# Router logits by float32 matmuls in four column tiles, on tokens that are not split in two

## The chip, the cores and the metric

The kernel runs on one core of a Trainium2 chip. The time is the device time of one execution in microseconds; three executions of the kernel before took 1358.14 to 1362.7 us, median 1361.56. The core's engines are TensorE (PE in the profile, its weight loads PEld), VectorE (DVE), ScalarE (ACT), GpSimd (POOL) and SyncE (SP, which here only issues transfers). Each works through its own queue in order; semaphores tie them.

## The reference

Two steps. The first is a causal average over 7 positions in each of 8 heads, with the softmax of a small table as weights:

```
x_pad = concat([zeros(B, 6, 192), x])                 # x is 8 x 3584 x 192
out[b,s,h,:] = sum_k softmax(weight)[h,k] * x_pad[b, s+k, h, :]
```

The second routes the 28672 results, called tokens, to 8 experts and applies a two-layer network:

```
logits = x @ w_gate                                   # 28672 x 8
for idx in argsort(-logits.flatten()):                # best pair first
    tok, e = idx // 8, idx % 8
    if assigned[tok] < 0 and counts[e] < 3584: assign tok to e
out[tokens of e] = relu(x[tokens of e] @ w1[e]) @ w2[e]   # 192 -> 1024 -> 192
```

Every token ends with exactly one expert, and every expert with 3584 tokens. Which expert a token gets hangs on comparisons between logits, so these have to be as exact as float32.

## The kernel before

**Attention and logits.** The tokens go in 16 batches of 1792 (half a sequence), 16 windows of 112 positions each. `load(i)` brings batch i into a tile X of 118 partitions (112 positions and the 6 before them); there are three such tiles, and the load for batch i+2 is issued on SP's queue at the top of batch i. `conv(i)` runs over the 8 heads h: one float32 matmul with a banded matrix TH into one of four PSUM banks "cv", then ACT copies the bank to the tile a (two of them), and after head 7 ACT's queue sends a to the scratch tensor attn in device memory. Between the matmul and the copy of each head, `mid(h)` puts the other work of the batch into the engines' queues:

- at h = 0 to 3, `transp(i-1, h)`: DVE transposes 32 x 32 blocks of a quarter of the batch before (a to aT), which puts features on partitions;
- at h = 2 to 5, `split(i-1, h-2)`: ACT rounds the quarter to the reduced format float32r (hi), and POOL, or DVE for the last quarter of some batches and in batch 15, subtracts (lo = aT - hi);
- at h = 0 and h = 4, `logits(i-2, 0)` and `(i-2, 1)`: 6 float32r matmuls of 512 columns each, hi with the table GH and lo with GL, all into one bank pl. GH holds the rounded gate weights in 32 columns and what the rounding left in another 32, so a bank has two halves that are added at the end.

After head 7, `end(i-2)` turns the logits round: ACT copies pl to L, PE transposes L in four pieces into a bank pt, DVE adds the two halves into the table LT with two operations, and `top` takes each token's best logit (M). Batch 15 is different: `transp_last` moves it in three thirds, and its logits come from plain float32 matmuls with the 32-column table GF (in the wk tile "c_mu"), six of 512 columns into partitions 0 to 31 of a bank.

**Routing** runs in the background, as generators whose steps `hook()` puts between the steps of the foreground. `half(0)` finds a threshold on the tokens seen so far by counting (`thresh`: DVE operations on X, m_x and t_t, and a small PE matmul per round), takes the first 8 batches, and makes lists of tokens for each expert: `sort` makes one-hot tiles oa on DVE (128 x 1024, bf16) and multiplies them on PE (128 matmuls bg<-X,oa), `gather` and `tokens` finish the list ia. The first expert tile's tokens are gathered with it (xg<-attn, on POOL's queue). `tail` does the logits of batch 14 and `tail2` those of batch 15, both after the last convolution, between the first expert matmuls; `half(1)`, `rest` and `last` route the remainder during the experts.

**What sets the order.** All queues are written in program order at build time; nothing is reordered on the chip. `hook` decides with a model of three clocks (`Meter`, `Pace`): every operation on PE, DVE and ACT adds an estimated time to its engine's clock, and a background step is put in when DVE's clock is not more than a slack ahead of PE's and what the step needs is past. So a change of what the model counts moves background steps to other places.

**Experts.** `FFN.run` goes over 56 tiles of 512 tokens: gather, transpose, `l1` (five float32r matmuls per 128 hidden units into ph), ReLU on ACT and the remainder on DVE (hh, hl), `l2` (into y), and a scatter. Weights are split once (`wsplit`: ACT rounds, POOL or DVE subtracts), which starts in batch 15 at heads 4 and 5, and written back to device memory for later use.

Of the kernel before, what the change touches and what calls it, by code (L numbers as in the profile page):

```python
# [5 lines left out]
F32 = mybir.dt.float32  # L6
# [21 lines left out]
class Meter:  # L28
# [5 lines left out]
    def __getattr__(self, op):  # L34
        f = getattr(self.eng, op)
        if op == "dma_start":
            return f

        def call(*a, **k):
            p = self.pace  # L40
            aps = [t for t in (*a, *k.values()) if hasattr(t, "shape") and hasattr(t, "dtype")]
            n = max(map(size, aps), default=0)
            bf = all(t.dtype == BF for t in aps if size(t) > 1)
            if self.name == "pe":
                n = size(aps[2])
# [7 lines left out]
            return f(*a, **k)  # L53

        return call
# [56 lines left out]
def build(ctx, tc, nc, x, weight, wg, attn, LT, wk):  # L112

    k = K()
# [44 lines left out]
    wgr = cst.tile([128, 6, 8], F32, name="wgr")  # L159
    GH = cst.tile([128, 6, 128], FR, name="GH")  # L160
    GL = cst.tile([128, 6, 128], FR, name="GL")
    GF = wk.tile([128, 6, 32], F32, name="c_mu")
    pm = wk.tile([128, 16], F32, name="pm")

    def gate_ops():
        for pb in range(4):
            nc.sync.dma_start(wgr[32 * pb:32 * pb + 32], wg.rearrange("(c f) e -> f c e", f=32))
        P.memset(GH.bitcast(F32), 0.0)
        P.memset(GL.bitcast(F32), 0.0)
        for pb in range(4):  # L170
            q = slice(32 * pb, 32 * pb + 32)
            P.tensor_copy(GH[q, :, 8 * pb:8 * pb + 8], wgr[q])
            P.tensor_copy(GL[q, :, 8 * pb:8 * pb + 8], wgr[q])
            P.tensor_tensor(GH[q, :, 32 + 8 * pb:40 + 8 * pb], wgr[q], GH[q, :, 8 * pb:8 * pb + 8].bitcast(F32),
                            op=OP.subtract)
        P.tensor_tensor(GF, GH[:, :, 0:32].bitcast(F32), GH[:, :, 32:64].bitcast(F32), op=OP.add)

# [33 lines left out]
    def transp(i, u):  # L211

        if u == 0:
            AT[i] = ([], k.hp[i % 2].tile([128, 16, 6, 32], FR, name="hi"),
                     k.hp[i % 2].tile([128, 16, 6, 32], FR, name="lo"))
        aT = k.tp.tile([128, 4, 6, 32], F32, name="aT%d" % u)
        V.transpose(aT.rearrange("p w c t -> p (w c t)"), AA[i][:, 4 * u:4 * u + 4].rearrange("p w d -> p (w d)"))
        AT[i][0].append(aT)
        if u == 3:
            AA.pop(i)  # L220

    def split(i, u, eng):
        aT = AT[i][0][u]
        hi, lo = (t[:, 4 * u:4 * u + 4] for t in AT[i][1:])
        A.activation(hi, aT, AF.Copy)
        eng.tensor_tensor(lo, aT, hi.bitcast(F32), op=OP.subtract)  # L226

# [7 lines left out]

    def logits(i, part):
        _, hi, lo = AT[i][0:3]
        if part == 0:
            AT[i] = (None, hi, lo, k.bank("pl"))
        pl = AT[i][3]  # L240
# [3 lines left out]
        if part:  # L244
            L = AT[i] = k.lrow()
            A.activation(L, pl[0:64], AF.Copy)

    def logits_last(u):
        i = NHB - 1
        if u == 0:  # L250
            AT[i].insert(0, k.bank("pl"))
        pl = AT[i][0]
        a = AT[i][1 + u].rearrange("p w (c t) -> p w c t", t=32)
        for c in range(2):
            PE.matmul(pl[0:32], GF[:, 2 * u + c], a[:, :, c], start=(u + c == 0), stop=(u + c == 3))
        if u == 2:
            L = AT[i] = k.lrow()
            A.activation(L[0:32], pl[0:32], AF.Copy)

    def logits_t(i):  # L260
        L = AT.pop(i)
        pt = k.bank("pt")
        last = i == NHB - 1
        n = 32 if last else 64
        for b in range(4):
            PE.transpose(pt[:, 64 * b:64 * b + n], L[0:n, 128 * b:128 * b + 128], k.ident[0:n, 0:n])
        v = pt[:, 0:256].rearrange("p (b s q e) -> p s e b q", s=2, q=4, e=8)
        o = LT[:, :, 16 * i:16 * i + 16].rearrange("p e (b q) -> p e b q", q=4)
        V.tensor_tensor(o, v[:, 0], pm.rearrange("p (b q) -> p b q", q=4)[:, None].to_broadcast([128, 8, 4, 4]),
                        op=OP.add)  # L270
        if not last:
            V.tensor_tensor(o, o, v[:, 1], op=OP.add)

    k.load, k.conv, k.transp, k.split, k.logits, k.logits_t = load, conv, transp, split, logits, logits_t
    k.toeplitz, k.gate_ops, k.transp_last, k.logits_last = toeplitz, gate_ops, transp_last, logits_last
    return k

# [1074 lines left out]
def moe_kernel(ctx, tc, x, weight, wg, w1, w2, out):  # L1352
# [6 lines left out]
    with ExitStack() as cw:  # L1359
# [46 lines left out]
        def tail():  # L1406

            k.logits(14, 0)
            k.logits(14, 1)
            yield PEA  # L1410
            end(14)
# [5 lines left out]
        def tail2():  # L1417
            for u in range(3):
                k.logits_last(u)
                yield PEA if u == 2 else None  # L1420
            end(15)
# [4 lines left out]
        bg.keep = 5  # L1426
        cs, c1, ct, ca, cl, cc = (ExitStack() for _ in range(6))
        cx = [ExitStack() for _ in range(3)]
# [3 lines left out]
        k.hp = [pool(cs, "hp0", 1, **right), pool(c1, "hp1", 1, **right)]  # L1432
        k.tp = pool(ct, "tp", 1, **right)
        k.ap = pool(ca, "ap", 2, **right)
# [5 lines left out]
        k.bank = lambda name: lps.tile([128, 512], F32, name=name)  # L1440
        k.lrow = lambda: lp.tile([64, 512], F32, name="L")

# [23 lines left out]
        for i in range(NHB):  # L1466
# [49 lines left out]
        end(13)  # L1516
        for c in (ca, ct, c1, cl):
            c.close()
        k.bank = lambda name: r.bg()
        k.lrow = lambda: oh.tile([64, 512], F32, name="oa")  # L1520
        ff.py = pool(cw, "py", 2, space=PSUM, **late)
# [66 lines left out]
```

## Time and profile before

| | |
|---|---|
| median of three runs | 1361.56 us (1358.14 to 1362.7) |
| the profiled execution | 1359.7 us, its span from first to last instruction 1357.9 us |
| PE, DVE, ACT, POOL busy | 94%, 78%, 43%, 47% of the span |
| hi on ACT, lo on POOL and DVE | 60 x 0.842, 50 x 1.893 and 10 x 1.648 us |
| transposes aT on DVE | 60 x 0.950 us |
| logit matmuls hi and lo of batches 0 to 13 | 84 and 84 |

Times in the profile are microseconds from the span's start. A row of a group names the line of the program (here nearly always 53, the helper that records every operation), engine, operation and tiles as out<-in, shapes, how often, busy time with the mean of one in ns, and the idle time of the engine just before with what ended it. PE's records overlap, since a matmul starts before the one ahead has ended: the mean is a latency, and what one costs is seen in how far apart they start. A float32 matmul leaves two records, one in float32r leaves one. A row of the timeline gives the start, the length of a merged stretch and how many records it holds. In the tables of stretches, the numbers after the engines' busy times are PE's granted clock as a share of full, the share of time in which the 16 transfer engines are busy, and GB/s.

### The profile page before, as it was taken

To read this page: it belongs to the slowest core of one execution; us is meant where nothing else is said; L and a number is where in the kernel's file an instruction comes from. 1 tells how busy PE (TensorE), PEld (TensorE's weight loads), DVE (VectorE), ACT (ScalarE), POOL (GpSimd) and SP (SyncE) were. 2 spreads that over 40 slices of the span, in tenths; PEclk is the share of its full clock that TensorE was granted. 3 is DMA by queue.
4 is the path that set the end of the run, shared out by engine and by line. 5 is a ranking of instruction groups with operands and counts; after the bars stand their busy time and mean duration, and the time that the engine had idled before them with its cause. 6 is when DMAs were issued, how large, how long until landed. Compare 5 with 4: busy or idle time off the path is not lost.

```text
span 1357.9 us, 20887 instructions
## 1 busy us (share of the span) xinstructions
PE 1282.5 (94%) x7351; PEld 1099.0 (81%) x7351; DVE 1055.2 (78%) x2248; ACT 587.7 (43%) x1242; POOL 636.1 (47%) x607
## 2 busy tenths in 40 slices
PE   5878896999889999999999999999999999999997
PEld 3544564788778898888889999999999999999997
DVE  7698964777999898898775777777777777777772
ACT  4655464357543444353324333333333333333332
POOL 5555557457664344344224434444443444444422
PEclk9988898999989999999989999999999999999999
DMA  9996569658764334324224241324322314141110
GB/s 228 287 257 191 167 211 297 206 176 288 258 224 155 122 110 144 134 94 139 78 71 145 95 173 58 101 91 145 100 87 85 101 47 145 45 146 41 42 33 28
DMA packets 114431, 188.23 MB, mean 139 GB/s; under 512 B 12352, under 2 KB 86544, under 8 KB 110096
## 3 DMA queue, kind: packets, MB, share of 16 engines
q1 hardware_dynamic: 63888, 120.75, 28.0%
q0 software_dynamic: 21504, 44.07, 10.6%
q10 hardware_dynamic: 28928, 22.02, 4.9%
q8 instruction: 59, 0.97, 0.3%
q14 instruction: 52, 0.43, 0.1%
HBM read 114.44 MB, written 72.35 MB: 138 GB/s over the span
## 4 chain that ended last, share of the span: by engine, by line
PE 73%; DVE 15%; DMA 4%; issue 3%; POOL 2%; ACT 2%; SPq 0%; POOLq 0%; DVEq 0%; ACTq 0%
PE ph L53 34%; PE y L53 33%; DVE X L53 4%; PE bg L53 3%; DMA attn<-a 2%; DVE aT L53 2%; DVE oa L53 2%; DVE hl L53 1%; PE cv L53 1%; DMA raw<-in_moe_w_dram 1%; POOL w L1187 1%; PE px L53 1%; DVE TH L53 1%; POOL xg L1206 1%; ACT hi L53 1%
## 5 line engine op out<-in xcount | busy, mean ns | idle before, releaser
L53 PE MATMUL y<-w,hh 128*128 128x384 f32 x1792 | 542.8, 358 | 0.0
L53 ACT ACTIVATE hh<-ph 128x512 fp32r<-128x512 f32 x448 | 267.6, 598 | 497.5 <-PE ph L53 497.4
L53 DVE SCALAR_TENSOR_TENSOR hl<-ph,hh 128x512 fp32r<-128x512 f32 x448 | 308.0, 688 | 185.1 <-ACT hh L53 181.4
L53 PE MATMUL y<-w,hl 128*128 128x192 f32 x1792 | 450.6, 251 | 0.0
L53 PE MATMUL ph<-xa,w 128*128 128x512 f32 x1344 | 399.1, 405 | 7.1 <-POOL w L1187 3.7
L53 PEld LDWEIGHTS y<-w,hh 128*128 128x128 f32 x1792 | 338.7, 189 | 25.2 <-issue 7.4
L53 PEld LDWEIGHTS y<-w,hl 128*128 128x128 f32 x1792 | 343.2, 192 | 15.3
L1274 POOL DMA_INDIRECT out_dram<-yo,ib x128 | 126.7, 990 | 295.6 <-DVE yo L53 280.7
L53 PEld LDWEIGHTS ph<-xa,w 128*128 128x128 f32 x1344 | 221.1, 191 | 29.2 <-DVE hl L53 4.0
L1274 POOL DMA_INDIRECT out_dram<-yo,ia x96 | 105.0, 1094 | 247.1 <-DVE yo L53 214.8
L53 DVE STREAM_TRANSPOSE xs<-xg 32x256 f32<-32x256 f32 (+1 forms) x512 | 188.8, 369 | 8.8
L53 PE MATMUL ph<-xd,w 128*128 128x512 f32 x448 | 179.2, 400 | 0.3 <-ACT w L53 0.3
L53 PE MATMUL ph<-xd,dl 128*128 128x512 f32 x448 | 175.8, 392 | 1.6 <-DVE dl L53 1.6
L1206 POOL DMA_INDIRECT xg<-attn,ib x128 | 129.5, 1012 | 40.1 <-issue 39.8
L226 POOL TENSOR_TENSOR lo<-aT,hi 128x768 fp32r<-128x768 f32 x50 | 93.3, 1893 | 74.4 <-ACT hi L53 74.4
L53 PE MATMUL cv<-X,TH 118*128 118x384 f32 x256 | 108.6, 558 | 18.9 <-DVE TH L53 12.4
L1206 POOL DMA_INDIRECT xg<-attn,ia x96 | 108.7, 1133 | 28.8 <-issue 24.3
L53 ACT ACTIVATE yt<-y 128x192 f32<-128x192 f32 x224 | 73.5, 328 | 109.0 <-PE y L53 107.4
L53 DVE TENSOR_TENSOR yo<-y,yt 128x192 f32<-128x192 f32 x224 | 79.5, 355 | 42.9 <-ACT yt L53 40.1
L53 PEld LDWEIGHTS cv<-X,TH 118*128 118x128 f32 x256 | 51.2, 213 | 65.5 <-issue 14.6
L53 PEld LDWEIGHTS ph<-xd,dl 128*128 128x128 f32 x448 | 84.9, 190 | 22.6 <-DVE dl L53 3.0
L53 PEld LDWEIGHTS ph<-xd,w 128*128 128x128 f32 x448 | 84.9, 190 | 21.1 <-issue 1.3
(243 smaller groups left out, 1191.7 us busy)
## 6 DMA issues: line engine op xcount, KB each, us to landing
w<-kw SPq DMA_DIRECT2D x16, 1536.0 KB
w<-kv SPq DMA_DIRECT2D x16, 1536.0 KB
X<-in_x_dram SPq DMA_DIRECT2D x16, 1344.0 KB
attn<-a ACTq DMA_DIRECT2D x16, 1344.0 KB
kw<-w SPq DMA_DIRECT2D x48, 256.0 KB
kv<-w SPq DMA_DIRECT2D x32, 384.0 KB
raw<-in_moe_w_dram SPq DMA_DIRECT2D x32, 192.0 KB
raw<-in_moe_w_dram SPq DMA_DIRECT2D x16, 256.0 KB
```

Source lines behind the costliest of these rows:

```text
L53: return f(*a, **k)
L226: eng.tensor_tensor(lo, aT, hi.bitcast(F32), op=OP.subtract)
L1187: eng.tensor_tensor(lo, r[0:n], hi[0:n].bitcast(F32), op=OP.subtract)
L1206: self.nc.gpsimd.indirect_dma_start(out=t[:, b], out_offset=None, in_=self.attn[0:rows], in_offset=bass.IndirectOffsetOnAxis(ap=idx[b], ax ...
L1274: st = nc.gpsimd.indirect_dma_start(out=self.out, out_offset=bass.IndirectOffsetOnAxis(ap=idx, axis=0), in_=o, in_offset=None, bounds_chec ...
```

## The change

Batches 0 to 14 are no longer split. The transposes write straight into one float32 tile aT per batch; hi, lo, the tables GH and GL, their pool, and the four splits are gone. GF, the 32-column table, now serves all batches. `logits(i, u)` takes feature block u of 6: four matmuls, one for each group of four windows, each 128 partitions by 32 weight columns with 128 tokens moving, and each writing its own 32 partitions of the bank (a column tile of the array). A batch has 24 of them, 12 at h = 2 and 12 at h = 5. The result has the four groups on four quarters of the partitions, so L is 128 x 128, one transpose turns it, and one DVE operation puts it into LT. Batch 15 uses the same function on its three thirds. The model of clocks counts such a matmul as a quarter of a float32 one, with its lower limit of 0.107 us.

```diff
-                d = n / 2400 * (1 if aps[2].dtype in (BF, FR) else 2 if op == "transpose" else 4)
+
+                d = n / 2400 * (1 if aps[2].dtype in (BF, FR) or size(aps[1]) == 32 else 2 if op == "transpose" else 4)
...
-        P.memset(GH.bitcast(F32), 0.0)
-        P.memset(GL.bitcast(F32), 0.0)
+        P.memset(GF, 0.0)
         for pb in range(4):
             q = slice(32 * pb, 32 * pb + 32)
...
+            P.tensor_copy(GF[q, :, 8 * pb:8 * pb + 8], wgr[q])
...
-        aT = k.tp.tile([128, 4, 6, 32], F32, name="aT%d" % u)
-        V.transpose(aT.rearrange("p w c t -> p (w c t)"), AA[i][:, 4 * u:4 * u + 4].rearrange("p w d -> p (w d)"))
-        AT[i][0].append(aT)
+            AT[i] = [k.hp[i % 2].tile([128, 16, 6, 32], F32, name="aT")]
+        V.transpose(AT[i][0][:, 4 * u:4 * u + 4].rearrange("p w c t -> p (w c t)"),
+                    AA[i][:, 4 * u:4 * u + 4].rearrange("p w d -> p (w d)"))
...
-    def split(i, u, eng):
-        aT = AT[i][0][u]
-        hi, lo = (t[:, 4 * u:4 * u + 4] for t in AT[i][1:])
-        A.activation(hi, aT, AF.Copy)
-        eng.tensor_tensor(lo, aT, hi.bitcast(F32), op=OP.subtract)
...
-        g, t = ((GH, hi), (GL, lo))[part]
-        for fb in range(6):
-            PE.matmul(pl, g[:, fb], t[:, :, fb, :], start=(part == 0 and fb == 0), stop=(part == 1 and fb == 5))
...
+        for c in range(4):
+            w = slice(4 * c, 4 * c + 4)
+            t = AT[i][u // 2].rearrange("p w (c t) -> p w c t", t=32)[:, w, u % 2] if i == NHB - 1 else AT[i][0][:, w, u]
+            PE.matmul(pl[32 * c:32 * c + 32, 0:128], GF[:, u], t, start=(u == 0), stop=(u == 5))
+        if u == 5:
             L = AT[i] = k.lrow()
-            A.activation(L, pl[0:64], AF.Copy)
...
+        PE.transpose(pt[:, 0:128], L, k.ident)
+        v = pt[:, 0:128].rearrange("p (b q e) -> p e b q", q=4, e=8)
         o = LT[:, :, 16 * i:16 * i + 16].rearrange("p e (b q) -> p e b q", q=4)
...
-                if i and 2 <= h < 6:
-                    k.split(i - 1, h - 2, V if h == 5 and (i < 6 or i == 14) or i == 15 else P)
-                if 2 <= i and h == (2 if i == 2 else 0):
-                    k.logits(i - 2, 0)
-                if 2 <= i and h == 4:
-                    k.logits(i - 2, 1)
+                if 2 <= i and h in (2, 5):
+                    for u in range(3):
+                        k.logits(i - 2, h // 4 * 3 + u)
```

How this stands in the queues. On PE, the end of routing's first half (the matmuls iq and c_oh, from which the list of tokens comes) before, at the start of batch 14; cv are the convolution's matmuls, pl the logits, px the transposes of the first expert tile:

```order
L53 MATMUL pl<-hi,GH 128x512 x6
L53 LDWEIGHTS ones
L53 MATMUL bg<-iq,ones 128x192
...
L53 MATMUL bg<-c_oh,X_1528 128x24
L53 MATMUL cv<-X,TH 128x384 x4
L53 MATMUL pl<-lo,GL 128x512 x6
L53 MATMUL cv<-X,TH 128x384 x3
L53 MATMUL pt<-ident,L 128x64 x4
L53 MATMUL cv<-X,TH 128x384
L53 MATMUL pl<-hi,GH 128x512 x6
```

and with the change, inside batch 15, up to the first expert tile:

```order
L54 MATMUL pl<-aT,c_mu 32x128 x12
L54 LDWEIGHTS ones
L54 MATMUL bg<-iq,ones 128x192
...
L54 MATMUL bg<-c_oh,X_1547 128x24
L54 MATMUL cv<-X,TH 128x384 x3
L54 MATMUL pl<-aT,c_mu 32x128 x12
L54 MATMUL cv<-X,TH 128x384 x2
L54 MATMUL px<-ident,xg 128x128 x4
```

Before, a whole batch follows iq ahead of px; now 5 convolution matmuls and 12 logit matmuls do. On POOL, where the last batch passes into the experts, before:

```order
L226 TENSOR_TENSOR lo<-aT_1635,hi 128x768
L1206 DMA xg<-attn,ia_105 128x192 x8
L1109 MEMSET dl 64x1024
L1187 TENSOR_TENSOR w_1763<-raw,w_1763 128x512
L1187 TENSOR_TENSOR dl<-raw,w_1763 64x512
```

and with the change:

```order
L1078 MEMSET dl 64x1024
L1156 TENSOR_TENSOR w_1629<-raw,w_1629 128x512
L1156 TENSOR_TENSOR dl<-raw,w_1629 64x512
L1175 DMA xg<-attn,ia_105 128x192 x8
L1156 TENSOR_TENSOR w_1629<-raw,w_1629 128x512
```

The subtraction lo is gone from POOL, and the memset and the first two weight splits now stand ahead of the eight gathers.

More of the change, by code (lines that the diff above doesn't have):

```diff
@@ L234, in transp_last, with logits @@
         AT[i] = AT[i] + [a] if u else [a]
[L236 to L240, printed above, removed]
-        g, t = ((GH, hi), (GL, lo))[part]
-        for fb in range(6):
-            PE.matmul(pl, g[:, fb], t[:, :, fb, :], start=(part == 0 and fb == 0), stop=(part == 1 and fb == 5))
-        if part:
-            L = AT[i] = k.lrow()
-            A.activation(L, pl[0:64], AF.Copy)
[L248 to L258, printed above, removed]
+    def logits(i, u):
+        if u == 0:
+            AT[i].append(k.bank("pl"))
+        pl = AT[i][-1]
+        for c in range(4):
[3 more added lines that the diff above has]
+        if u == 5:
+            L = AT[i] = k.lrow()
+            A.activation(L, pl[:, 0:128], AF.Copy)
     def logits_t(i):
@@ L262, in logits_t @@
         pt = k.bank("pt")
[L263 to L267, printed above, removed]
-        o = LT[:, :, 16 * i:16 * i + 16].rearrange("p e (b q) -> p e b q", q=4)
[L269 to L275, printed above, removed]
+        PE.transpose(pt[:, 0:128], L, k.ident)
+        v = pt[:, 0:128].rearrange("p (b q e) -> p e b q", q=4, e=8)
+        o = LT[:, :, 16 * i:16 * i + 16].rearrange("p e (b q) -> p e b q", q=4)
+        V.tensor_tensor(o, v, pm.rearrange("p (b q) -> p b q", q=4)[:, None].to_broadcast([128, 8, 4, 4]), op=OP.add)
+    k.load, k.conv, k.transp, k.logits, k.logits_t = load, conv, transp, logits, logits_t
+    k.toeplitz, k.gate_ops, k.transp_last = toeplitz, gate_ops, transp_last
     return k
@@ L1406, in tail @@
         def tail():
-            k.logits(14, 0)
-            k.logits(14, 1)
-            yield PEA
+            for u in range(6):
+                k.logits(14, u)
+                if u % 2:
+                    yield PEA if u == 5 else None
             end(14)
@@ L1417, in tail2 @@
         def tail2():
-            for u in range(3):
-                k.logits_last(u)
-                yield PEA if u == 2 else None
+            for u in range(6):
+                k.logits(15, u)
+                if u % 2:
+                    yield PEA if u == 5 else None
             end(15)
@@ L1426, in moe_kernel @@
         bg.keep = 5
-        cs, c1, ct, ca, cl, cc = (ExitStack() for _ in range(6))
+        cs, c1, ca, cl, cc = (ExitStack() for _ in range(5))
         cx = [ExitStack() for _ in range(3)]
```

16 lines of the change are left out of this document (3 added, 13 removed).

## The prediction

> **What bounds the kernel now.** I read first the page's 40 slices of 34 us, for where the engines are full, and then the same by stages.
>
> ```profile
> span 1357.9 us, 20887 instructions
> PE   5878896999889999999999999999999999999997
> DVE  7698964777999898898775777777777777777772
> PEclk9988898999989999999989999999999999999999
> DMA  9996569658764334324224241324322314141110
> ```
>
> ```profile
> 12.00:75.00 63.00, 56.45 (x180) 33.28 (x181) 42.19 (x82) 38.08 (x76) 38.30 (x53) 0.97 1.05 279
> 75.00:205.00 130.00, 107.88 (x487) 68.03 (x486) 112.95 (x186) 72.46 (x138) 73.80 (x44) 0.87 0.69 202
> 205.00:285.00 80.00, 68.11 (x417) 51.84 (x416) 50.80 (x101) 31.52 (x63) 45.90 (x41) 0.91 0.74 240
> 285.00:1357.90 1072.90, 1050.07 (x6274) 945.83 (x6273) 841.54 (x1856) 439.78 (x952) 473.37 (x454) 0.99 0.35 115
> ```
>
> The columns are the stretch, its length, busy time of PE, weight loads, DVE, ACT and POOL, then the granted clock, the DMA share and GB/s. From 285 us on PE is busy 1050 of 1073 us: the expert stage is PE's, and this change leaves it alone. So what is won or lost comes before 285 us. There, 12 to 75 us has DMA full (share 1.05, 279 GB/s), and 75 to 205 us has DMA down to 202 GB/s, PE with gaps at clock 0.87, and DVE busy 113 of 130 us. The loads of x mark the batches: the load for batch i+2 is issued when the convolution of batch i-1 ends, so these three rows are the starts of batches 2, 5 and 13.
>
> ```profile
> 28.25 0.27 SPq L194 DMA_DIRECT2D X<-in_x_dram  x1
> 58.23 0.27 SPq L197 DMA_DIRECT2D X<-in_x_dram  x1
> 170.31 0.27 SPq L197 DMA_DIRECT2D X<-in_x_dram  x1
> 204.53 0.66 PE L53 MATMUL px<-ident,xg 128*128 128x128 f32 x4 [1.60 <-ACT a L53]
> X<-in_x_dram SPq DMA_DIRECT2D x16, 1344.0 KB
> attn<-a ACTq DMA_DIRECT2D x16, 1344.0 KB
> ```
>
> Batches 2 to 4 take (58.2 - 28.3) / 3 = 10.0 us each, batches 5 to 12 take (170.3 - 58.2) / 8 = 14.0 us, batches 13 to 15 end on PE at 204.5 - 1.6 = 202.9, so 32.6 us together. A batch moves 2 x 1344 KB and a 70 KB piece of x, 2.82 MB; at 290 GB/s (between the 279 above and the peak slice) that is 9.7 us. Batches 2 to 4 run at that pace. Batches 5 to 12 do not, and there the question is who holds them.
>
> ```profile
> ACT hi L53 <- DVE aT L53: 11.2, 6, 2.8
> PE bg L53 <- DVE m_x L53: 10.2, 3, 3.8
> L53 DVE TENSOR_TENSOR oa<-irep,q 128x1024 bf16<-128x1024 bf16 x16 | 19.6, 1263 | 0.7 <-PE bg L53 0.7
> L53 DVE TENSOR_TENSOR oa<-irep,q 128x1024 bf16<-128x1024 bf16 x33 | 21.0, 681 | 0.0
> L53 DVE TENSOR_SCALAR X<-X,t_t 128x576 bf16<-128x576 bf16 x6 | 7.5, 1298 | 0.0
> L53 DVE TENSOR_SCALAR X<-X,t_t 128x384 bf16<-128x384 bf16 x9 | 2.3, 313 | 0.1
> L53 DVE SCALAR_TENSOR_TENSOR t_t<-t_u,t_t 128x1 f32<-128x1 f32 x12 | 7.3, 636 | 0.3
> L53 DVE TENSOR_REDUCE t_u<-t_mx 128x1 f32<-128x3 f32 x5 | 0.8, 156 | 0.2
> L53 DVE TENSOR_TENSOR lo<-aT,hi 128x768 fp32r<-128x768 f32 x5 | 5.4, 1103 | 0.3 <-ACT hi L53 0.3
> L53 DVE TENSOR_TENSOR LT<-LT,pt 128x128 f32<-128x128 f32 x9 | 2.6, 287 | 0.3
> L226 POOL TENSOR_TENSOR lo<-aT,hi 128x768 fp32r<-128x768 f32 x50 | 93.3, 1893 | 74.4 <-ACT hi L53 74.4
> L53 ACT ACTIVATE hi<-aT 128x768 fp32r<-128x768 f32 x60 | 50.5, 842 | 22.3 <-DVE aT L53 22.3
> ```
>
> (Waits are of 75 to 125 us; the oa row of 16 is of 75 to 206 us, that of 33 from 285 us on.) DVE sets the pace in two ways. Its own work is long, and partly swollen: the same oa takes 1263 ns here and 681 later, and an operation on one element per partition takes 636 ns where a neighbour takes 156. POOL runs lo for 93 us in just this stage, so I read the swelling as DVE waiting while POOL works; the trace shows the coincidence, not the cause. And DVE is tied into PE's path through ACT: hi of the batch before stands in ACT's queue between the evacuations a<-cv, so a late transpose stops them, and four banks later PE.
>
> **The change part by part.**
>
> *Removed.* All 60 hi on ACT (50.5 us), all 50 lo on POOL (93.3) and 10 on DVE, the second LT addition, and the tie just named: ACT keeps only a<-cv and L, and what waits for aT is now a matmul two thirds of a batch later. In 75 to 205 us DVE loses 5.4 (lo) and 2.6 (LT), and if the swelling is POOL's, 16 x (1.263 - 0.681) = 9.3 from oa, 6 x (1.298 - 0.313 x 1.5) = 5.0 and 12 x (0.636 - 0.156) = 5.8 from the threshold: 28 us of its 113. That leaves 85 us for some 10.5 batches, 8.1 each, under DMA's 9.7. If the swelling stays it is 105, 10.0 each, 0.3 over DMA's pace and 2.4 us over eight batches. So DVE falls to about DMA's pace or below it either way.
>
> *Added on PE.* Six passes hi and six lo per batch, 128 columns wide, become 24 float32 matmuls of 32 by 128, in the trace two records each, 48 records.
>
> ```profile
> 186.37 1.42 PE pl L53 x6
> 19.43 5.40 PE L53 MATMUL cv<-X,TH 118*128 118x384 f32 x16 [0.38 <-DVE TH L53]
> 237.42 3.62 PE L53 MATMUL bg<-X,c_mu 128*32 128x512 f32 x8
> 237.88 0.11 PEld L53 LDWEIGHTS bg<-X,c_mu 128*32 128x32 f32 x1 [0.32 <-issue]
> 205.03 0.60 PE L53 MATMUL bg<-ident,xg 128*64 128x128 f32 x4
> 363.89 0.20 PE L53 MATMUL bg<-onesf,r_c 128*8 128x1 f32 x2
> 180.39 1.65 PE L53 MATMUL bg<-X,oa 128*128 128x16 bf16 x24
> L53 PE MATMUL bg<-onesf,r_c 128*8 128x1 f32 x14 | 1.4, 166 | 0.0
> ```
>
> Now: the convolution is (5.40 - 0.49) / 15 = 0.327 a record, 5.2 us for 16, its own latency of 0.49 taken off. Logits are 2 x 1.42 = 2.84, four transposes about 0.4: 8.5 us a batch. No row shows four column tiles at once. Upper bound: one after the other, as the 128-column float32 records of ident,xg come, (0.60 - 0.27) / 3 = 0.109 apart, 48 x 0.109 = 5.2 us. Lower bound: as near as two float32 records ever follow here, 0.20 - 0.166 = 0.03, 48 x 0.032 = 1.5 us. The two are far apart and the four tiles write four different quarters of the partitions, so I take the middle by ratio, 2.8 us. One transpose is 0.15 and I allow 0.4 for changing between whole array and tiles: 8.55 us a batch. PE's load thus stays as it was, 8.5, and under DMA's 9.7.
>
> [...]
>
> *Moved.* The planner puts the first half of routing one batch later: sorting (128 matmuls oa at (1.65 - 0.21) / 23 = 0.063, 8 us) from batches 12 and 13 to 13 and 14, its end from the start of batch 14 into batch 15. On POOL two weight splits now stand ahead of the first eight gathers.
>
> *Sum against the profiled 1359.7 us.* Batches 0 to 4 are DMA's and stay. Batches 5 to 12 at 9.7 are 77.6 instead of 112.1: -34.5. Batches 13 and 14 at 8.55 + 4.0 and 15 at 8.55 + 2.0 are 35.7 instead of 32.6: +3.1. PE waited 10.2 us for the threshold's m_x in its order; I leave about half, +6. Stage: -25.4. After it, the logits of batches 14 and 15 stand on PE's path between the first experts' matmuls: 2.84 and 12 x 3.62 / 8 = 5.4 become 2 x 2.8, -2.6. Nothing else in PE's 1050 us moves. Sum -28, so 1331.7 in the profile's own time; the median of the runs is 1.9 above that execution, which gives 1334.
>
> **The rivals.** *The tiles do not run side by side* (the change not doing what it says). 5.2 us of logits make a batch 10.95: batches 2 to 4 +2.9, 5 to 12 are 87.6 (-24.5), 13 to 15 are 42.9 (+10.3), stalls +6, after the stage 10.4 - 8.2 = +2.2. Sum -3, 1358 us. For it: every float32 record in the trace pays its columns in full. Against: those all use the same columns of the array.
>
> *Each record waits for its own weights*, on the slower side. Place: the 768 records, 672 in the 14 batches and 96 after; price 0.11 + 0.107 = 0.217 each, 10.4 a batch, which is then 16.1: batches 2 to 4 +18, 5 to 12 +17, 13 to 15 +26, after the stage 20.8 - 8.2 = +13. 1436 us. It decides from 0.113 us a record, where the gain of 3 us above is used up. Against it: eight c_mu records with their own 0.11 us loads come (3.62 - 0.59) / 7 = 0.43 apart, and 512 columns at the 0.109 of 128 would be 0.436, so there the loads are hidden.
>
> [...]
>
> *The late list gives back part.* The first gather needs the list, which in this order ends with 5 convolutions and 12 logit matmuls to go, 5.3 us.
>
> ```profile
> 187.63 0.26 PE L53 MATMUL bg<-iq,ones 128*128 128x192 bf16 x1
> 190.11 0.19 DVE L53 SCALAR_TENSOR_TENSOR ia<-m_j,m_x 128x32 int32<-128x32 int32 x1
> PEld ph L53 <- POOL w L1187: 4.0, 1, 4.0
> xg<-attn,ia POOLq DMA_INDIRECT x96, 2.8
> ```
>
> From that iq matmul to the list is 2.7 us, four gathers at about 1.3 are 5.2, landing 2.8: 10.7 us, so PE stands idle 5.4. Against: the two splits ahead of the gathers can take away PE's 4.0 us wait for POOL's w, which is why the sum has neither. With the full 13 us of threshold stalls instead of 6 it is +12: 1346 us.
>
> *DMA's pace to the end.* If sorting hides too, batches 5 to 15 at 9.7 are 106.7 instead of 144.7; with -2.6 and the 4.0 of w that is -45, 1317 us. Against: PE's 12.6 in batches 13 and 14.
>
> **How the numbers follow.** The forecast 0.40 (1324 to 1344 on its own), late list 0.28, no overlap 0.18, DMA's pace 0.10, waiting for weights 0.04. The three faster cases are 0.78. No overlap lies about the edge of 0.3% (4 us, what a measurement of this kernel tells from nothing): 0.07 faster, 0.08 the same, 0.03 slower. So faster 0.85, same 0.08, slower 0.07. The range runs from just below DMA's pace to just below no overlap, 1315 to 1357, leaving out half of that case, the weights and a little below.
>
> **What would show it.** The starts of batches 5 to 13 by the loads of x, 9.7 apart instead of 14.0, with DMA at 280 GB/s or more until the convolutions end near 177 us; oa at about 0.68 us and t_t at 0.16 in that stage (else the swelling was not POOL's); logit records 0.06 us apart (0.03 to 0.11 are the bounds); PE's wait for xg after the last convolution; the stretch from the first ph matmul on the same to 5 us. Wrong would make it: records over 0.113 us, the clock falling below 0.87 as PE's gaps change, or batches staying near 14 us with DVE no longer busy.

## The result and the profile after

The changed kernel takes 1326.04 us (median of 1321.26 to 1330.83) beside 1362.13 us for the kernel before: a ratio of 0.9743, 95% interval 0.9724 to 0.9762, 36 us less. Timed a second time, beside the experiments below, it took 1320.93 us and the ratio was 0.9712 (0.9688 to 0.9736). The forecast was 1334, range 1315 to 1357.

The profiled execution took 1324.88 us, its span 1323.1. First the page's span and its slices of PE, DVE and DMA, then the stages of the changed kernel (columns as before: PE, weight loads, DVE, ACT, POOL, clock, DMA share, GB/s).

```profile
span 1323.1 us, 21760 instructions
PE   5888959999799999999999999999999999999997
DVE  7369648779999988899757777777777777777772
DMA  9999879488753433424222341432323222141100
```

```profile
12.00:75.00 63.00, 52.35 (x353) 28.01 (x352) 32.84 (x79) 25.41 (x59) 6.15 (x27) 0.92 0.98 282
75.00:175.00 100.00, 84.30 (x774) 50.16 (x772) 73.55 (x165) 41.49 (x95) 7.94 (x10) 0.92 0.94 271
250.00:1323.00 1073.00, 1050.28 (x6257) 946.43 (x6256) 840.48 (x1854) 438.42 (x951) 473.85 (x452) 0.99 0.35 115
```

The last row is the expert stage: PE busy 1050 of 1073 us, as before to 0.3 us. The middle row is what was 130 us long with DMA at 202 GB/s and POOL busy for 73.8: now 100 us at 271 GB/s, POOL all but idle. The loads of x, the end of the convolutions and the list behind them, from the timeline (start, us, queue or engine, operation):

```profile
57.73 0.27 SPq L191 DMA_DIRECT2D X<-in_x_dram  x1
137.35 0.27 SPq L191 DMA_DIRECT2D X<-in_x_dram  x1
168.69 0.81 PE L54 MATMUL cv<-X,TH 118*128 118x384 f32 x2
164.54 0.26 PE L54 MATMUL bg<-iq,ones 128*128 128x192 bf16 x1
167.02 0.19 DVE L54 SCALAR_TENSOR_TENSOR ia<-m_j,m_x 128x32 int32<-128x32 int32 x1
167.11 1.29 POOL L1156 TENSOR_TENSOR w<-raw,w 128x512 fp32r<-128x512 f32 x1 [42.39 <-ACT w L54]
168.95 1.26 POOL L1156 TENSOR_TENSOR dl<-raw,w 64x512 fp32r<-64x512 f32 x1 [0.55 <-ACT w L54]
170.39 1.25 POOL L1175 DMA_INDIRECT xg<-attn,ia  x1 [0.17 <-issue]
179.50 1.75 PE L54 MATMUL px<-ident,xg 128*128 128x128 f32 x4 [9.99 <-DMA xg<-attn,ia]
```

Batches 5 to 12 take (137.35 - 57.73) / 8 = 9.95 us each, where they took 14.0. The convolutions end at 169.5 instead of 202.9: 33.4 us won in the stage. Then PE stands for 10.0 us until the first expert tile's tokens have come; before, it stood 1.6. Of the span's 34.8 us, nothing more than 1.4 comes from behind the stage.

What ends the waits in the stage (75 to 169 us; engine, tile, releaser: us in total, times, longest):

```profile
ACT a L54 <- DMA attn<-a: 21.5, 5, 7.3
PE cv L54 <- ACT a L54: 8.8, 3, 4.3
PE bg L54 <- DVE m_x L54: 0.2, 1, 0.2
```

Now ACT waits for the store of the tile a from two batches ago, whose buffer it writes next, and through ACT so does PE. That is how the DMA bound of this stage looks from the engines. The waits for DVE's m_x, 13.1 us in the stage before, are 0.2.

### The profile page after: what moved, and what is told of

Its sections match the earlier page's. It is cut to its first block, busy times and chain, and to the rows that moved or that the text cites. A ratio compares the mean times of both kernels' runs of the same rounds, so it can differ in the third digit from the quotient of the medians.

```text
span 1323.1 us, 21760 instructions
## 1 busy us (share of the span) xinstructions
PE 1251.3 (95%) x7879; PEld 1077.4 (81%) x7879; DVE 1005.2 (76%) x2223; ACT 543.2 (41%) x1182; POOL 540.1 (41%) x547
## 4 chain that ended last, share of the span: by engine, by line
PE 77%; DVE 9%; DMA 8%; issue 2%; POOL 2%; ACT 2%; SPq 1%; POOLq 0%; ACTq 0%; DVEq 0%
PE ph L54 34%; PE y L54 33%; DMA attn<-a 5%; PE cv L54 4%; PE bg L54 3%; DMA raw<-in_moe_w_dram 3%; DVE X L54 2%; DVE hl L54 2%; PE px L54 1%; PE pl L54 1%; DVE TH L54 1%; DVE oa L54 1%; POOL xg L1175 1%; POOL w L1156 1%; DVE r_w L54 0%
## 5 line engine op out<-in xcount | busy, mean ns | idle before, releaser
L54 PE MATMUL ph<-xd,dl 128*128 128x512 f32 x448 | 175.8, 392 | 1.2 <-DVE dl L54 1.2
L54 PE MATMUL cv<-X,TH 118*128 118x384 f32 x256 | 103.8, 539 | 31.1 <-ACT a L54 18.4
L54 PEld LDWEIGHTS cv<-X,TH 118*128 118x128 f32 x256 | 48.0, 206 | 66.0 <-ACT a L54 26.7
L54 ACT ACTIVATE a<-cv 128x384 f32<-128x384 f32 x128 | 59.2, 491 | 66.2 <-DMA attn<-a 36.8
```

## The experiments

All are the changed kernel with one thing altered. They were timed in three groups, each beside runs of the kernel before (medians 1360.3, 1358.6 and 1359.5 us); the second timing of the change belongs to the last group. The ratio to hold theirs against is 0.9712 to 0.9743 (1321 to 1326 us).

| altered | median, us | ratio (95%) | batches 5 to 12, us each | last convolution ends |
|---|---|---|---|---|
| nothing (first, second profile) | 1326.0, 1320.9 | 0.9743, 0.9712 | 9.95, 9.4 | 169.5, 166.5 |
| lo on POOL again | 1335.9 | 0.9823 (0.9787 to 0.9859) | 10.4 | 185.0 |
| hi on ACT again | 1331.2 | 0.9781 (0.9752 to 0.9810) | 9.6 | 170.4 |
| both again | 1350.7 | 0.9930 (0.9904 to 0.9957) | 10.8 | 193.7 |
| memsets on POOL | 1323.3 | 0.9741 (0.9716 to 0.9765) | 9.4 | 165.5 |
| tiles in another order | 1329.4 | 0.9785 (0.9752 to 0.9818) | 9.7 | 172.5 |
| one column tile | 1363.4 | 1.0024 (1.0008 to 1.0040) | 11.7 | 203.7 |
| attn stored twice | 1380.0 | 1.0155 (1.0128 to 1.0182) | 13.2 | 216.9 |
| gathers ahead of splits | 1323.2 | 0.9723 (0.9700 to 0.9746) | 9.5 | 167.6 |
| slack 2.5 | 1316.4 | 0.9677 (0.9654 to 0.9700) | 10.7 | 170.4 |
| slack 3 | 1322.9 | 0.9717 (0.9695 to 0.9739) | 11.0 | 174.1 |
| slack 4 | 1323.6 | 0.9749 (0.9728 to 0.9770) | 11.0 | 176.2 |

(The last two columns are of the profiled execution: the first convolution matmuls of batches 5 and 13, and the start of the last one plus its 0.5 us. Between the two profiles of the unaltered kernel they move by 0.5 us a batch and 3 us.)

### Does POOL slow DVE?

```diff
+    def split(i, u, pool):                     # at the places of before
+        aT = AT[i][0][:, 4 * u:4 * u + 4]
...
+        if LO and pool:
+            k.nc.nc.gpsimd.tensor_tensor(k.lo[:, s], aT, k.hi[:, s].bitcast(F32) if HI else aT, op=OP.subtract)
```

> The changed kernel with the 50 subtractions of 128x768 put back on POOL, at the places where the kernel before had them, as dead work: they read the transposed tokens and write a tile that nobody reads. The order on every other engine is unchanged. Theory (POOL's work slows DVE): oa in the stage from 75 us on goes back from 0.68 to about 1.26 us, the 576-wide X from 0.36 to about 1.3, t_t from 0.16 to about 0.64; that puts some 1.9 us a batch on DVE's 7.3, 9.2 in all, just under the 9.95 of a batch now, so the time rises little, 0 to 10 us. Rival (the slow DVE rows came from something else that the change removed, ACT's hi or the waits): the rows stay at 0.68, 0.36 and 0.16 and the time within 3 us.

DVE's groups in 75 to 171 us, of the changed kernel and then with lo on POOL (busy, mean ns, idle before):

```profile
L54 DVE TENSOR_TENSOR oa<-irep,q 128x1024 bf16<-128x1024 bf16 x16 | 10.0, 681 | 0.0
L54 DVE TENSOR_SCALAR X<-X,t_t 128x576 bf16<-128x576 bf16 x6 | 1.8, 360 | 0.0
L54 DVE SCALAR_TENSOR_TENSOR t_t<-t_u,t_t 128x1 f32<-128x1 f32 x12 | 1.6, 157 | 0.3
```

```profile
L54 DVE TENSOR_TENSOR oa<-irep,q 128x1024 bf16<-128x1024 bf16 x16 | 12.9, 858 | 0.0
L54 DVE TENSOR_SCALAR X<-X,t_t 128x576 bf16<-128x576 bf16 x6 | 4.2, 753 | 0.0
L223 POOL TENSOR_TENSOR lo<-aT 128x768 fp32r<-128x768 f32 x33 | 50.7, 1561 | 37.4 <-DVE aT L54 35.2 <-DVE t_mx L54 2.3
```

oa and X are slow again, t_t is not, and the price is 10 to 15 us, above what was expected. The means hide two kinds of operations. Of the 16 oa, 13 ran while no lo did and took 678 ns on average; 3 ran under a lo and took 1638. An operation kept its time or waited for POOL's to end: in the kernel before, the six long oa (1970 to 2333 ns) end 0.55 us after a lo does and the four long t_t (1534 to 1665 ns) 0.02 us after, and one oa that had started 0.17 us ahead of its lo kept 644 ns. Here t_t was untouched because none of its twelve fell under a lo. That makes the swelling a matter of where the two happen to meet, and most of the price falls in batches 13 to 15, where DVE makes oa for the sort: they take 185.0 - 140.4 = 44.6 us instead of 32.3.

> As the run with the 50 subtractions put back on POOL, but each is replaced by a copy of one element per partition of the transposed tokens (so that it waits for the same transpose) and a memset of 128x1536, some 1.4 us: POOL is busy as long as with lo (1.53 us) and at the same places, but writes only and reads nothing for that time. Theory (what stops DVE is that both read SBUF: operations with two inputs from SBUF, oa and t_t, stood while POOL read, and reduces, transposes and operations on PSUM did not): oa stays at 0.68 us and t_t at 0.16 even where a memset runs; the 576-wide X, a bf16 tensor_scalar with one input, may still be held. Time within 4 us of the changed kernel, where lo cost 11. Rival (DVE stands whenever POOL works, whatever it does): oa and X are held up to the end of the memset as in the run with lo, and the time rises by 8 to 12 us.

```diff
-            k.nc.nc.gpsimd.tensor_tensor(k.lo[:, s], aT, ...)
+            P.tensor_copy(k.lo[:, 4 * u, 0, 0:1], AT[i][0][:, 4 * u, 0, 0:1])
+            P.memset(k.lo.rearrange("p w c t -> p (w c t)")[:, 1536 * (u // 2):1536 * (u // 2) + 1536], 0.0)
```

The same groups with memsets on POOL:

```profile
L219 POOL MEMSET lo<- 128x1536 f32 x32 | 44.2, 1383 | 1.9
L54 DVE TENSOR_TENSOR oa<-irep,q 128x1024 bf16<-128x1024 bf16 x16 | 10.0, 697 | 0.0
L54 DVE TENSOR_SCALAR X<-X,t_t 128x576 bf16<-128x576 bf16 x6 | 3.5, 643 | 0.0
L54 DVE SCALAR_TENSOR_TENSOR t_t<-t_u,t_t 128x1 f32<-128x1 f32 x11 | 1.5, 156 | 0.2
```

POOL is busy nearly as long, and oa and t_t keep their times: 10 oa ran wholly or in part under a memset, at 709 ns on average (the longest 977). No t_t took more than 160 ns. Still longer than in the changed kernel are tensor_scalars: X at 643 ns (360 there), c_f at 1282 (169), c_oh at 1161 (271). The time is that of the changed kernel. So it is not POOL's being busy that holds oa: under a lo 3 of them took 1638 ns on average, under a memset 10 took 709, and of the two only lo reads.

### The tie through ACT, and both together

> The changed kernel with the 60 copies hi of 128x768 put back on ACT, between the evacuations where the kernel before had them, as dead work that nobody reads; the order of everything else is unchanged. Theory (the tie: a copy that waits for its transpose holds up the evacuations behind it, and so PE): waits of ACT's hi for DVE's aT of 8 us or more in 75 to 169 us come back, the convolutions come later, and batches 5 to 12 go from 9.95 to 10.5 to 11.5 us, the time up by 5 to 15 us; the DVE rows stay as fast as they are. Rival (DVE's load alone set the 14 us): DVE is no longer late, so the copies find their transposes done and cost nothing beyond ACT's own 34 us in 100 that were idle: time within 3 us.

```diff
+        if HI:
+            k.nc.nc.scalar.activation(k.hi[:, s], aT, AF.Copy)
```

Waits of ACT with hi back (75 to 169 us):

```profile
ACT a L54 <- DMA attn<-a: 15.7, 5, 4.5
ACT hi L221 <- DVE aT L54: 5.4, 3, 3.1
```

The batches stay at 9.6 us and the convolutions end where they ended. Once DVE is quick, hi rarely waits for a transpose (5.4 us in three waits, not 8 or more), and ACT still waits mostly for the store. So the tie alone costs these batches nothing, where the theory had them at 10.5 to 11.5. The time is 5 to 10 us up, at the edge of what the intervals tell apart, which the rival (within 3) didn't have either. None of it lies in batches 5 to 12; in this profile PE waits 11.6 us for xg instead of 10.0, and the rest of it wasn't located.

> The changed kernel with both kinds of dead work put back, 60 hi on ACT and 50 lo on POOL that read them; only the logits' matmuls and the few tiny DVE operations remain changed. Theory (slow DVE and the tie together made the 14 us): each makes the other worse, batches 5 to 12 come back to 12 to 14 us, and the time rises by 18 to 33 us, to 1344 to 1359. Rival (the gain comes from the fewer matmul passes on PE): the batches stay near 10 us and the time rises by less than 8 us.

The edit is both of the above, hi feeding lo. DVE's groups again, 75 to 171 us, and two waits of 75 to 169 us:

```profile
L54 DVE TENSOR_TENSOR oa<-irep,q 128x1024 bf16<-128x1024 bf16 x10 | 12.9, 1343 | 0.0
L54 DVE SCALAR_TENSOR_TENSOR t_t<-t_u,t_t 128x1 f32<-128x1 f32 x12 | 7.5, 647 | 0.3
L54 DVE TENSOR_REDUCE t_u<-t_mx 128x1 f32<-128x3 f32 x5 | 0.8, 156 | 0.2
L54 DVE STREAM_TRANSPOSE aT<-a 128x768 f32<-128x768 f32 x31 | 28.1, 949 | 0.0
```

```profile
ACT hi L221 <- DVE aT L54: 23.8, 10, 4.4
POOL lo L223 <- ACT hi L221: 32.9, 11, 5.3
```

25 to 30 us of the gain are gone, more than the two alone add up to (15 to 25). oa is at 1.34 us and t_t at 0.65, the values of the kernel before, while reduces and transposes, which read one input, keep 0.156 and 0.95 under the same lo. Now the ring closes: lo holds DVE, DVE's transposes are late, hi waits for them (23.8 us), and the evacuations behind hi wait too.

Batches 5 to 12 take 10.8 us, where 12 to 14 were expected and 14.0 were the pace before. The two cannot be held against each other as they stand: before, 13 of the sort's 16 oa lie in batch 12, and in this run all 16 lie in batches 13 to 15. Batches 5 to 15 hold the whole sort in each of these kernels. They took 144.1 us before, 111.9 with the change (108.3 in its second profile), and 133.8 here, so about two thirds of the gain is given back. DVE was busy for 122.9 of the 144.1 us and 115.4 of the 133.8, against 82.0 of 111.9 with the change. The last 10 us weren't tried by themselves: this run leaves out DVE's own lo and second LT addition (8.0 us by the prediction's rows), and the logits' dearer matmuls and their wait for hi and lo.

### Do the four column tiles run at once?

> The changed kernel with the logits' matmuls in another order: three for one column tile, then three for the next, so that neighbours use the same columns (in the last two batches, after the convolutions, the order is kept). Same instructions, same result. Theory (the four column tiles run at once, and that is why the logits cost 1.3 us a batch): records within a tile come 0.109 us apart, a batch's 24 pl matmuls take about 4.4 us instead of 1.3 to 1.5, PE's load of a batch goes from about 7.1 to 10.2 us, just over the 9.95, and batches 13 to 15, which PE bounds, take 3 us more each: the time rises by 6 to 14 us. Rival (float32 records of 32 rows of output are cheap in any order): no change, within 3 us, records nearer than 0.06 us.

```diff
-                    for u in range(3):
-                        k.logits(i - 2, h // 4 * 3 + u)
+                    for c in range(4):
+                        for u in range(3):
+                            k.logits(i - 2, h // 4 * 3 + u, (c,))
```

Half a batch's logits on PE's timeline, with the convolution matmul before, of the changed kernel, then with three matmuls of one tile in a row:

```profile
119.46 0.49 PE L54 MATMUL cv<-X,TH 118*128 118x384 f32 x1
119.87 0.86 PE L54 MATMUL pl<-aT,c_mu 128*32 128x128 f32 x24
```

```profile
98.72 0.49 PE L54 MATMUL cv<-X,TH 118*128 118x384 f32 x1
99.14 1.59 PE L54 MATMUL pl<-aT,c_mu 128*32 128x128 f32 x24
```

In the changed kernel four records start within 0.02 us, and the next four 0.109 after them: 24 records in 0.86 - 0.27 = 0.59 us from first start to last (a record's own 0.27 taken off), four tiles at the speed of one. So it is in 24 of the 28 halves; the other four take 1.09. In the other order it is 1.59 - 0.27 = 1.32, not the 2.2 that was expected: a tile's records follow each other 0.109 apart, but the next tile's begin while these are still running, so some two tiles overlap. So PE got 1.46 us a batch more, not 3, and batches 5 to 12 stayed at 9.7: the slack under DMA took it. The time is 3 to 8 us up, where 6 to 14 were expected, and the test of the price was too weak.

> The changed kernel without column tiles: the same float32 logits, from the same unsplit transposed tokens, as six matmuls of 512 columns into one tile of 32 columns (12 records of 0.43 us, 5.2 us a batch instead of 1.2), four small transposes instead of one; every other instruction stands where it stood. Theory (the tiles run at once and this is worth 4 us of PE a batch): PE was busy 84 us of the 100 in which ten batches now run, so a batch comes to 12.4 us against DMA's 9.95: batches 5 to 12 +16 to 20, batches 13 to 15 +8, the logits of batches 14 and 15 behind the stage +8; with what batches 2 to 4 and the stalls give, 20 to 36 us slower, ratio 0.989 to 1.001. Rival (PE has that room, since part of its 84 us is waiting, and DMA still sets the pace): only batches 13 to 15 and the last two logits pay, 8 to 16 us, ratio 0.980 to 0.986.

```diff
-        for c in range(4):
...
-            PE.matmul(pl[32 * c:32 * c + 32, 0:128], GF[:, u], t, start=(u == 0), stop=(u == 5))
+        t = ... AT[i][0][:, :, u]
+        nc.nc.tensor.matmul(pl[0:32], GF[:, u], t, start=(u == 0), stop=(u == 5))
```

Half a batch's logits with one tile, and the stretch that was the middle row above:

```profile
96.84 2.76 PE L228 MATMUL pl<-aT,c_mu 128*32 128x512 f32 x6
```

```profile
75.00:175.00 100.00, 100.00 (x349) 40.13 (x348) 60.88 (x135) 36.38 (x77) 1.95 (x5) 1.00 0.79 243
```

Six records 0.434 apart, 2.2 us for half a batch instead of 0.59. PE is busy 100 of 100 us, DMA falls to 243 GB/s, a batch takes 11.7 us, and the time is that of the kernel before, 0.2% above it. This is just above the theory's range, and its lesson is sharp: dropping the splits without the tiles would have won nothing, since PE would have become the bound. With the splits left in as dead work and the tiles used, 10 us are won. Only both together give 36.

### What sets the pace now?

> The changed kernel with the convolved tokens of every batch stored a second time, into a scratch tensor that nobody reads, by SP's queue: 1344 KB more for each batch. Theory (DMA sets the pace of batches 2 to 12 now, 9.95 us for 2.82 MB, 283 GB/s): a batch takes 4.16 MB / 283 = 14.7 us, 4.75 more; eleven batches and part of the last three make 52 to 65 us, so 1378 to 1391. Rival (PE or DVE sets the pace at 9.95 and DMA only keeps up): DMA has less than 1 us a batch free, so a part is still seen, but 280 GB/s is exceeded or the time rises by less than 30 us.

```diff
+        k.nc.nc.sync.dma_start(k.attn2[i % 2 * 1792:(i % 2 + 1) * 1792].rearrange("(w p) d -> p w d", p=W), a[0:W])
```

```profile
75.00:173.00 98.00, 69.94 (x508) 36.42 (x509) 49.18 (x117) 29.18 (x71) 1.94 (x5) 0.86 1.05 318
```

54 to 59 us more, inside the theory's range; PE and DVE have more idle time than in the changed kernel. But DMA moved 318 GB/s here, against 271 and 281 in the two profiles of the changed kernel, and a batch grew by 3.2 to 3.7 us, not 4.75. The rival's sign, more than 280 GB/s, came as well, but not its time (less than 30 us). So the transfers do set the pace, and yet a batch of 9.95 us, 2.82 MB, is 283 GB/s: a tenth or more of the 318 reached here goes unused. Where it is lost, no run shows. Of the 47 us by which the convolutions end later, batches 5 to 12 make 26, and batches 2 to 4 and 13 to 15 about 11 each.

### The late list

> The changed kernel with the two weight splits that POOL makes between the list and the first gather moved behind the first tile's four gathers. Theory (PE's 10 us wait after the last convolution is list 167.0, splits 3.2, four gathers 5.2, landing 4.1 one after the other): the first gather is issued 3.2 us earlier, PE's wait for xg falls from 10.0 to about 6.8 us and the time falls by 3 us, ratio to the kernel before 0.972. Rival (the splits are needed as much): PE waits as long for w on POOL instead, no change.

```diff
-                if i == 15 and h in (4, 5):
-                    ff.wsplit(-1, P)
...
                 first(0)
+                for _ in range(2):
+                    ff.wsplit(-1, P)
                 first(1)
```

Ratio 0.9723, between the two values of the unaltered kernel: no gain that can be told. The first gather went out 2.2 us after the list where it had been 3.4, and PE's wait came in two parts:

```profile
170.43 0.30 PE L54 MATMUL px<-ident,xg 128*128 128x128 f32 x1 [2.82 <-DMA xg<-attn,ia]
175.78 0.98 PE L54 MATMUL px<-ident,xg 128*128 128x128 f32 x3 [5.05 <-DMA xg<-attn,ia]
```

2.82 + 5.05 = 7.9 us, 2 less than the 10.0 of the changed kernel (9.6 in its second profile), not 3.2 less. PE did not wait for w instead, so the theory's direction holds. What is left is mostly the landing. The first gather went out at 167.3, ahead of the last batch's store of attn (168.7), and PE had it at 170.4, 3.1 us later. The second went out at 168.9, just behind that store, and PE had it at 175.8, 6.9 us later. From 170 to 173.5 us the store's queue moved 1.08 MB and the gathers' queue nothing.

> The changed kernel with the planner's slack (how far it lets the routing's DVE work run behind PE's clock) at 2.5 us instead of 1.5: the routing's first half ends with 13 convolutions to go instead of 5. Theory (the late list alone makes the 10 us wait): the list is there some 8 us before the last convolution, PE's wait for xg falls from 10.0 to under 2 us, the convolutions end within 2 us of 169.5, and the time falls by 6 to 10 us, ratio about 0.968. Rival (what the list is given earlier, PE pays in waits for DVE inside the stage): the convolutions end 4 to 8 us later, time within 4 us of the changed kernel.

> The same with the slack at 4 us: the list ends with 22 convolutions to go. Theory: as with 2.5, px follows the last convolution at once, and since the routing's matmuls lie in batches that DMA paces anyway (10 us against PE's 7), batches 13 to 15 get shorter too: the convolutions end at 166 to 169 us, time 8 to 13 us below the changed kernel, ratio 0.965 to 0.968. Rival: with DVE 4 us behind, PE waits for the threshold's counts at each step (9 steps of up to 2.5 us more) and all of the gain is given back: time within 4 us.

> The planner's slack at 3 us, between 2.5 (list with 13 convolutions to go, 1316 us) and 4 (22 to go, 1324 us): 21 convolutions to go. Theory (the list wants to be early, the sort wants to stay out of batches 11 and 12, where it cost 5 us with slack 4): much like 4, 1320 to 1325, since the list ends in the same batch. Rival: the gain behind the stage with slack 4 (no wait for xg) comes with fewer stalls, 1308 to 1314, the best of all.

> The changed kernel itself, once more beside the kernel before, so that the other runs stand against more than four of its times: 0.9743 again, between 0.972 and 0.977.

```diff
-            bg.hook(1.5)
+            bg.hook(2.5)        # and 3, 4
```

The first tile's transposes with slack 2.5, then with 4:

```profile
170.19 0.30 PE L54 MATMUL px<-ident,xg 128*128 128x128 f32 x1
173.85 1.04 PE L54 MATMUL px<-ident,xg 128*128 128x128 f32 x3 [3.36 <-DMA xg<-attn,ia]
```

```profile
174.63 1.56 PE L54 MATMUL cv<-X,TH 118*128 118x384 f32 x4
176.02 0.63 PE L54 MATMUL px<-ident,xg 128*128 128x128 f32 x4
```

The wait for xg does go: 10.0, then 3.4 (under 2 was expected), then none. The 3.4 is again a gather behind a store: it went out at 164.1, just after the store of batch 14 (163.9), and landed 9.7 us later. What is given back in the stage grows as the wait goes, while the sort moves into batches 12 and 13 (slack 2.5), then 11 and 12: the convolutions end at 170.4, with slack 3 at 174.1, with 4 at 176.2. With 2.5 the median is 1316.4 us, 4.5 below the second timing of the unaltered kernel, and the ratio 0.9677 against 0.9712; the two are of different groups. The intervals still touch (0.9700 and 0.9688), so that is the best version seen but not a settled gain. With 3 and 4 nothing is left, as the theory for 3 and the rival for 4 said. The rival's reason did not come with its number: with slack 4 PE waits only 0.7 us for m_x, and what makes the convolutions late there wasn't found.

The unaltered kernel's second ratio, 0.9712, lies below the 0.972 to 0.977 that was expected. Two timings of one kernel thus differ by 0.003, and a difference of that size between runs here means nothing.

## Why the prediction was right

The forecast was 8 us above the first timing and 13 above the second; its range held both. Against the profiled execution the sum was -28 and the span shows -34.8: stage -33.4 instead of -25.4, behind it -1.4 instead of -2.6. In the stage, batches 5 to 12 gave -32.4, batches 13 to 15 +0.2, and the start -1.2.

**What bounds the kernel before: DVE, right, and in the main shown.** The swelling is POOL's: put back, lo brings oa to 1.34 and t_t to 0.65 us, and a memset in its place does not. "The coincidence, not the cause" can be dropped. The trace of the kernel before had it already, operation by operation: 9 of its 16 oa met no lo and took 671 ns on average, and 7 ran under one and took 2025. One row was misread: 93 us is lo's time on POOL in the whole kernel, and 65.7 of it lies in 75 to 205 us. The second of the two ways, the tie through ACT, is hardly there before: of PE's 22.0 us of waits in that stretch, 19.1 are ended by DVE itself (m_x, oa, c_bi) and 2.9 by ACT. With hi and lo both back PE does wait for ACT, 8.1 us for L, which stands behind hi; with hi alone the tie costs batches 5 to 12 nothing.

**Batches 5 to 12 at DMA's pace, -34.5: right in kind.** (137.2 - 57.6) is 79.6 us where 77.6 was forecast, 9.95 a batch, and 9.4 in the second profile. oa at 0.68 and t_t at 0.16 were named as the sign and came. DMA at "280 GB/s or more" was 271 and 281.

**Logits on PE, 2.8 us a batch: mis-sized.** The step that failed is the bounds. "As near as two float32 records ever follow here", 0.03 us, was taken as the lower end, from records that use the same columns; with four tiles they are 0.109 / 4 = 0.027 apart on average, so 48 of them come to 1.3 us (2 x 0.59 = 1.2 from first start to last), below the lower end of 1.5. Here the price was the one-tile spacing divided by the number of tiles; the middle by ratio had no ground.

**Changing between array and tiles, 0.4: right.** The 0.4 was an allowance that no row of the kernel before showed. In the changed kernel, from the last cv to the first pl 0.41 us pass, where cv follows cv after 0.327, and the same 0.09 is lost on the way back; four changes make 0.36. Rival two, 1436 us, had each record wait for its own weights. The trace disagrees: of the 24 loads of half a batch, 0.11 us each and 2.6 us in all, the 0.59 us between the first pl and the last show nothing (weight loads of pl in 75 to 171 us; ns, min, median, max):

```profile
L54 PEld LDWEIGHTS pl<-aT,c_mu x432: 105/110/178, 78.5 to 167.6; 128*32 128x32 f32 x144
```

**Batches 13 to 15, +3.1: too dark by the logits.** The last three batches took 32.3 us, 32.1 before; with logits at 1.2 instead of 2.8 the sum for them is 35.7 - 3 x 1.6 = 30.9.

**Threshold stalls, +6: wrong.** PE's waits for m_x are 0.2 us. The sum kept half of them as a matter of PE's order. They came from DVE standing under POOL: lo put back on POOL alone brings nearly all of them back (the kernel before in 75 to 205 us, then lo on POOL in 75 to 169):

```profile
PE bg L53 <- DVE m_x L53: 13.1, 4, 3.8
PE bg L54 <- DVE m_x L54: 12.1, 4, 4.3
```

**The late list, put among the rivals, happened, but by another chain.** The forecast chain was 10.7 us from iq to the landed gathers, with 5.3 covered by convolutions. It took 15.0, from iq at 164.5 to px at 179.5, with 5.0 covered. The list took its 2.7; 3.2 passed between the list and the first gather, which were the splits that the rival had counted only as a gain. The remaining 9.1 is not four gathers one after the other and a landing of 2.8. PE's first transpose needs the first gather alone, and that one took 9.1 us from its issue at 170.39 to px. The last store of attn had been issued 0.3 us before it, and until that store was two thirds through, the gathers' queue hardly moved. Here is the changed kernel: the store's issue; then the packets, MB and share of the store's queue (q10) and of the gathers' (q0) from 170.4 to 176 us; then the gathers issued in that window and, for comparison, those of 250 to 600 us, with the median us to landing:

```profile
170.06 0.31 ACTq L203 DMA_DIRECT2D attn<-a  x1
q10 hardware_dynamic: 1179, 0.91, 59.2%
q0 software_dynamic: 2, 0.01, 0.4%
xg<-attn,ia POOLq DMA_INDIRECT x5, 7.8
xg<-attn,ia POOLq DMA_INDIRECT x65, 2.7
```

The weights' transfers (q1) took another 38.2% of the 16 engines' time in this window; in the run with the gathers ahead of the splits only the store ran from 170 to 173.5 us, and the gathers' queue stood as well.

**Behind the stage, -2.6 forecast, -1.4 measured: luck.** The wait for xg costs 8.4 us more than the wait at that place before. PE's wait for POOL's w, 3.7 us, is gone, as the rival's counter-argument had it, and the logits of batches 14 and 15 take 1.25 + 1.40 = 2.65 instead of 8.2, -5.6. That makes -0.9 of the -1.4, out of terms of which only a part of the last was in the sum. So the named sign missed: from the first ph matmul on the kernel is 10.5 us shorter (1141.1 for 1151.6), not the same to 5. The late-list rival's 1346 did not come because these terms took its cost back, and the stage had won more than the sum said.

**DMA's pace to the end, 1317, given 0.10, was about as near as the forecast.** Batches 5 to 15 took 111.9 us, 108.3 in the second profile; that rival had 106.7, and the forecast 77.6 + 35.7 + 6 = 119.3. So most of the sort does hide.

**No overlap, 1358: the rival's price was near**, though its case was not. The kernel with one tile is that rival: 1363.4 us, a batch at 11.7 for 10.95.

## What to carry to other kernels

Before moving an elementwise operation to POOL, look at which DVE operations will run at the same time: here oa, with two inputs from SBUF, took 2025 ns on average where it met POOL's lo and 671 where it did not. The cost showed as a mean too long for its shape, oa at 1263 ns in the stage and 681 among the experts, while reduces beside it kept 156 and transposes 950. When work is taken off one engine and put on another, price the receiving engine first: here the splits were worth nothing until the logits fitted on PE under DMA's pace. A wait should leave the sum with its cause: the threshold's stalls were DVE's under POOL, and went with POOL's work. And look at what large transfer is issued just before a small one that is waited for: here the gathers behind a store landed 7 to 10 us after their issue, where 2.7 is the median among the experts.

## What the runs showed of the hardware

- Four float32 matmuls of 128 x 32 weights in four column tiles start within 0.02 us of each other, and the next four 0.109 us later: four times the rate of one tile, weight loads included. So it was in 24 of the 28 halves. With three matmuls in a row on one tile, the next tile's still overlapped: 24 records in 1.32 us, where 0.109 apart would make 2.5.
- A DVE operation on one element per partition (t_t) took 157 ns alone and up to 1857 ns with POOL's subtraction back behind hi, itself 1935 ns on average; in the kernel before the four long ones, up to 1665 ns, ended 0.02 us after it. A reduce beside it took 156 either way.
- A second store of 1344 KB a batch raised DMA from 271 and 281 to 318 GB/s and the time by 54 to 59 us: this stage was paced by transfers, and still left a tenth or more of that rate unused.
- Gathers issued from 0.3 us behind a 1344 KB store on moved 0.01 of the 1.53 MB of the next 5.6 us, and the first was in PE's hands after 9.1 us.
